# An attention layer in front of a folded two-matrix network: the first unit's inputs, means and head steps are moved

## The chip, the cores and the metric

The kernel runs on one core of a Trainium2 chip. The time is the device time of one execution in microseconds (us): 539.33 us as the median of three runs (539.18 to 541.11). The execution that the profiler recorded took 540.83 us, of which 539.0 us are the span from its first to its last instruction.

## The reference

```python
# attention: q, k, v are [4, 8, 768, 64]
k_sum = k.reshape(B, H, 24, 32, 64).max(axis=3)       # 24 summary keys per head
v_sum = v.reshape(B, H, 24, 32, 64).mean(axis=3)      # 24 summary values per head
scores_l = q @ k.T / 8, kept where |row - column| < 16, else -1e9
scores_s = q @ k_sum.T / 8 + log(32)
a = softmax(concatenate([scores_l, scores_s]))
x = (a @ concatenate([v, v_sum])).transpose(0, 2, 1, 3).reshape(3072, 512)
# network: w1, w2 [512, 1024], w3 [1024, 1024], w_out [1024, 512], all float64
out = ((x @ w1) * (x @ w2)) @ w3 @ w_out              # [3072, 512]
```

## The kernel before, in words

The 3072 tokens are six units of 512 tokens. Of each unit the eight heads are four pairs, so there are 24 pair steps. A pair step on TensorE is scores (`sc`, L319: queries against a window of 160 keys and 24 summary keys), then a softmax on the other engines, transposes of the softmax (`tp`, L373), and outputs (`po`, L393: against the values and the summary means). `keep_x` (L401) splits an output into a high and a low part for the network. The network per unit is two gate products, multiplied (`gate`, L409), and a projection with wp = w3 @ w_out (`project`, L444).

wp is made first: `fold_weights` (L192) needs all of w3 and w_out. Weights arrive as float64. `convert` (L152) turns a piece into a high and a low float32r part: an ACT step per 512 columns (L167), a shift (L175) and a bit merge (L178) on DVE, a rounding cast on ACT (L188), and the difference on DVE (L109). A fold product is three matmuls of 512 columns; a row x6 in the order is the two products that one w_out tile makes with one w3 tile. In the order, `w_106` to `w_357` are the four tiles of w_out, `w_115` to `w_196` are the first four tiles of w3, and `w_415`, `w_536`, `w_666`, `w_807` are the last four. `w_895` and later are w1 and w2.

What sets the order: SP and PE follow the program text (a manual schedule), ACT, DVE and POOL a list scheduler with priorities. The program text is a loop over steps t, one step for each weight piece that is begun. `LOADS` and `WORK` are tables of what is loaded and done at which step, `FIRST` gives the step at which a pair of the first two units begins, and `run` hands out fold and network matmuls up to a number of columns. From pair 8 on, a second loop puts two pairs at a time into the network's matmuls, in "slots" of transposes, scores, outputs. All input loads stand on SP's queue in order. A load into a buffer still in use waits there, and everything behind it waits too.

PSUM banks: `mm` 2 (gates, fold), `tp` 2 (transposes, outputs, and the accumulators of the third and fourth block of wp), `sc` 4. `ring` is ten SBUF buffers for raw weights, raw keys, values' rows and `h`.

Of the kernel before, what the change touches and what calls it, by code (L numbers as in the profile page):

```python
# [30 lines left out]
FIRST = (15, 18, 20, 22, 27, 32, 37, 44)  # L31
# [4 lines left out]
    *(("wo", 0, 0), ("w3", 0, 0), ("wo", 0, 1), ("w3", 1, 0), ("wo", 1), ("w3", 2, 0), ("w3", 3, 0)),  # L36
    *(("w3", 0, 1), ("w3", 1, 1), ("wo", 2), ("w3", 2, 1), ("w3", 3, 1), ("wo", 3)),
# [10 lines left out]
NORMALIZE = "VAAAAAAA"  # L48
SECOND = "AAAVAVVA"
# [21 lines left out]
def attention_moe(ctx, tc, qG, kW, kT, vP, vW, vB, mask, w1, w2, w3T, wo, out):  # L71
    nc = tc.nc
    B, NPAIR, _, S = kT.shape
    NB = S // BLOCK
# [20 lines left out]
    ident = const.tile([P, P], F32, name="ident")  # L95
    make_identity(nc, ident)
    mask_sb = const.tile([P, 3, KR], F32, name="mask_sb")


    mean_sb = sb.tile([P, S // P, P], F32, name="mean_sb", tag="v", bufs=2)  # L100
    nc.gpsimd.memset(mean_sb, 0.0)
    for i in range(P // BLOCK):
        for at in (CUT, CUT - 64):
            part = mean_sb.rearrange("p t n -> p (t n)")[i * BLOCK : (i + 1) * BLOCK, at + i :: P + P // BLOCK]
            nc.gpsimd.memset(part[:, : S // P], 1.0 / BLOCK)
# [22 lines left out]
    def weight(name, i, src, shape, part=None):  # L128

        n = src.shape[1] // 2  # L130
        parts = range(n // PIECE) if part is None else [part]
        units.append((name, i, shape, list(parts), len(todo) + len(parts) - 1))
        for k in parts:
            todo.append(src[:, 2 * k * PIECE : 2 * (k + 1) * PIECE])

    def start_loads(at_least):

        while todo or due_loads:
            if len(loading) >= at_least and len(loading) + len(working) + len(kraws) + len(vraws) + made[0] + 2 >= RING:
                return  # L140
            if due_loads:
                due_loads.pop(0)()
                continue
            if len(loading) >= AHEAD:
                return
            raw = sb.tile([P, 2 * PIECE], U32, name="wraw", tag="ring", bufs=RING)
            nc.sync.dma_start(raw, todo.pop(0))
            loading.append(raw)
            due_loads.extend(LOADS.pop(begun[0], ()))
            begun[0] += 1  # L150

    def convert(name, i, shape, parts, last):  # L152


        n = len(parts) * PIECE
# [6 lines left out]
        for k in range(len(parts)):  # L162
# [13 lines left out]
        for k, low_word in enumerate(low_words):  # L176
            some = bits[:, k * PIECE : (k + 1) * PIECE]
# [8 lines left out]
        at = parts[0] * PIECE  # L186
# [4 lines left out]
        have.update((name, i, part) for part in parts)  # L191

    def fold_weights(order):
        acc = {}
        for i, j in order:
            while not {("w3", i, j * P // PIECE), ("wo", j // 2, j % 2 * DO // PIECE)} <= have:
                yield 0
# [25 lines left out]
    def load_keys(b, p):  # L223
        raw = sb.tile([P, S], F32, name="raw", **held(b))
# [32 lines left out]
    def mean_products(tiles):  # L257
        po = ps.tile([P, 512], F32, name="means", tag="sc", bufs=4)
        for i in range(S // P):
            nc.tensor.matmul(  # L260
                po[:KR, :DM],
                lhsT=mean_sb[:, i, :KR],
                rhs=tiles[i // 2][:, i % 2],
                start=i == 0,
                stop=i == S // P - 1,
            )
        return po
# [17 lines left out]
    def load_sums(u, p, v):  # L285
        for b, blocks, n in batches(u):
            for g, at in enumerate((CUT, CUT - 64)):
# [4 lines left out]
                else:  # L292
                    src = vs[b][at : at + NB, p * P : (p + 1) * P]
                    nc.gpsimd.tensor_copy(to, src.unsqueeze(1).broadcast_to([NB, n, P]))

    def load_scores(u, p):
# [4 lines left out]
        nc.sync.dma_start(k, kW[p, :, u * NBLK : (u + 1) * NBLK])  # L301
        return q, k

# [108 lines left out]
    def gate(f, x, hs):  # L412
        acc = []
        for w in range(2):
# [6 lines left out]
            for c in range(NC):  # L421
                while (GATES[w], k, c * FQ // PIECE) not in have:
# [132 lines left out]
    def first_pair(s):  # L555
# [34 lines left out]
    def means():  # L590
        po = mean_products(vraws)
        vraws.clear()
        vs[0] = sb.tile([KR, DM], F32, name="vs0", tag="pt", bufs=6)
        nc.scalar.copy(vs[0], po[:KR, :DM])

    LOADS = {
        7: [lambda: nc.sync.dma_start(mask_sb, mask)],
        8: [lambda: rows(1)],
        11: [lambda: fetch(0)],
        12: [lambda: keys(1)],  # L600
        13: [lambda: keys(0)],
        14: [lambda: rows(0)],
        15: [lambda: rows(2), lambda: fetch_values(0)],
        16: [lambda: fetch(1)],
        18: [lambda: keys(3)],
        21: [lambda: fetch(2), lambda: fetch_values(1)],
        22: [lambda: keys(2)],
        24: [lambda: fetch(3)],
        25: [lambda: fetch_values(2)],
        28: [lambda: fetch_values(3)],  # L610
    }
    WORK = {
        13: [lambda: summaries(0, 0, kraws.pop(0)), lambda: fill(0)],
        14: [means, lambda: summaries(0, 1, kraws.pop(1)), lambda: fill(1)],
        19: [lambda: fetch_sums(0)],
        20: [lambda: load_second(0), lambda: load_second(3), lambda: summaries(0, 2, kraws.pop(2)), lambda: fill(2)],
        21: [lambda: load_second(1), lambda: summaries(0, 3, kraws.pop(3)), lambda: fill(3), lambda: fetch_sums(1)],
        22: [lambda: load_second(4), lambda: fetch(4), lambda: fetch_sums(2)],
        23: [lambda: second_batch(0), lambda: load_second(2)],
        24: [lambda: second_batch(1), lambda: fetch(5)],  # L620
        25: [lambda: second_batch(3), lambda: second_batch(4)],
        26: [lambda: second_batch(2), lambda: load_second(5)],
        27: [lambda: second_batch(5), lambda: load_second(6), lambda: fetch(6), lambda: fill(4), lambda: fill(5)],
        28: [lambda: fetch_sums(3)],
        29: [lambda: fetch_values(4), lambda: fetch_sums(4)],
        31: [lambda: load_second(7)],
        32: [lambda: second_batch(6)],
        37: [lambda: second_batch(7), lambda: fetch_values(5), lambda: fetch(7), lambda: fill(6), lambda: fetch_sums(5)],
        40: [lambda: fill(7)],
        42: [lambda: fetch_values(6)],  # L630
        43: [lambda: fetch_sums(6)],
# [143 lines left out]
```

## Time and profile before

| what | value |
|---|---|
| median of the runs | 539.33 us |
| the profiled execution / its span | 540.83 us / 539.0 us |
| PE busy, DVE busy, ACT busy, POOL busy | 517.9, 237.5, 238.9, 56.3 us |
| network's first matmul on PE | 88.9 us |
| end of PE's last matmul | 535.5 us |

TensorE is busy for 96% of the span, and its clock is granted at full speed but for two short stretches in the first 60 us. To read the profile, look at the first 90 us apart from the rest: in the rest PE hardly ever waits. A matmul's busy time in the page overlaps its neighbours', so rates are read from a long row of a chain or timeline divided by its count.

### The profile page before, as it was taken

To read this page: it belongs to the slowest core of one execution; us is meant where nothing else is said; L and a number is where in the kernel's file an instruction comes from. 1 tells how busy PE (TensorE), PEld (TensorE's weight loads), DVE (VectorE), ACT (ScalarE), POOL (GpSimd) and SP (SyncE) were. 2 spreads that over 40 slices of the span, in tenths; PEclk is the share of its full clock that TensorE was granted. 3 is DMA by queue.
4 is the path that set the end of the run, shared out by engine and by line. 5 is a ranking of instruction groups with operands and counts; after the bars stand their busy time and mean duration, and the time that the engine had idled before them with its cause. 6 is when DMAs were issued, how large, how long until landed. Compare 5 with 4: busy or idle time off the path is not lost.

```text
span 539.0 us, 9912 instructions
## 1 busy us (share of the span) xinstructions
PE 517.9 (96%) x3852; PEld 421.8 (78%) x3852; DVE 237.5 (44%) x686; ACT 238.9 (44%) x688; POOL 56.3 (10%) x103
## 2 busy tenths in 40 slices
PE   2897999999999999999999999999999999999997
PEld 1655777888788888888888888888888888888885
DVE  5868889999503226724244033252042351122210
ACT  5547898887345225226235144253162261222210
POOL 1001221111001101103003002011021020000000
PEclk9988899999999999999999999999999999999999
DMA  8999689956524005544032141050160020000001
GB/s 309 403 348 350 189 270 369 280 183 197 167 96 154 0 1 169 162 128 135 0 111 60 40 152 58 0 157 33 40 190 1 1 75 39 21 21 0 1 19 58
DMA packets 30574, 67.21 MB, mean 125 GB/s; under 512 B 4032, under 2 KB 7616, under 8 KB 30528
## 3 DMA queue, kind: packets, MB, share of 16 engines
q1 hardware_dynamic: 27072, 60.30, 35.2%
q10 hardware_dynamic: 3456, 6.29, 3.1%
q8 instruction: 30, 0.49, 0.4%
q14 instruction: 16, 0.13, 0.1%
HBM read 58.51 MB, written 6.29 MB: 120 GB/s over the span
## 4 chain that ended last, share of the span: by engine, by line
PE 91%; DVE 3%; ACT 3%; DMA 1%; issue 1%; POOL 0%; SPq 0%; POOLq 0%; ACTq 0%
PE mm L113 79%; PE po L393 5%; PE sc L319 4%; PE tp L373 2%; DVE w L109 1%; DMA wraw<-in_w3T_dram 1%; DVE wf L178 1%; ACT w L188 1%; PE means L260 1%; ACT sm L347 1%; DVE wf L175 1%; ACT wf L167 0%; ACT wp L211 0%; DVE wp L109 0%; POOL k L306 0%
## 5 line engine op out<-in xcount | busy, mean ns | idle before, releaser
L113 PE MATMUL mm<-x,w 128*128 128x512 f32 x1152 | 264.9, 390 | 0.0
L113 PEld LDWEIGHTS mm<-x,w 128*128 128x128 f32 x1152 | 215.4, 188 | 45.6 <-issue 0.5
L113 PE MATMUL mm<-wp,h 128*128 128x512 f32 x576 | 133.9, 391 | 0.0
L113 PEld LDWEIGHTS mm<-wp,h 128*128 128x128 f32 x576 | 107.5, 188 | 22.7 <-issue 0.2
L347 ACT ACTIVATE sm<-sm,mx 128x120 f32<-128x120 f32 x192 | 73.6, 387 | 19.9 <-DVE mx L333 19.9
L438 DVE TENSOR_TENSOR g<-mm,g 128x512 f32<-128x512 f32 x48 | 33.1, 689 | 90.6 <-PE mm L113 88.7
L439 ACT CAST h<-g 128x512 fp32r<-128x512 f32 x48 | 29.6, 618 | 87.7 <-DVE g L438 87.7
L113 PE MATMUL mm<-w,w 128*128 128x512 f32 x192 | 54.1, 435 | 12.6 <-ACT w L188 11.5
L113 PEld LDWEIGHTS mm<-w,w 128*128 128x128 f32 x192 | 38.2, 206 | 25.6 <-ACT w L188 13.3
L457 ACT COPY o<-mm 128x512 f32<-128x512 f32 x24 | 14.1, 585 | 81.3 <-PE mm L113 81.3
L109 DVE TENSOR_TENSOR h<-g,h 128x512 fp32r<-128x512 f32 x48 | 35.7, 743 | 24.2 <-ACT h L439 24.0
L435 ACT COPY g<-mm 128x512 f32<-128x512 f32 x48 | 28.0, 584 | 35.6 <-PE mm L113 35.2
L333 DVE CUSTOM_DVE_ANT_0 sm<-sc,mask_sb 128x120 f32<-128x120 f32 x192 | 41.0, 275 | 5.5 <-PE sc L319 5.5
L382 DVE COPY pt<-tp 120x512 f32<-120x512 f32 x19 | 12.4, 686 | 67.7 <-PE tp L373 67.7
L306 POOL COPY k<-ks 128x96 f32<-128x96 f32 (+1 forms) x32 | 10.1, 327 | 252.3 <-DMA k<-in_kW_dram 210.0
L347 ACT ACTIVATION_READ_ACCUMULATOR sm<-sm,mx 128x1 f32 x192 | 36.5, 190 | 0.0
L109 DVE TENSOR_TENSOR x<-po,x 128x512 fp32r<-128x512 f32 x24 | 16.6, 690 | 42.2 <-ACT x L404 42.2
L356 POOL TENSOR_TENSOR sm<-sm,mx 128x960 f32<-128x960 f32 x16 | 29.1, 1820 | 6.0 <-DVE mx L353 5.0
L167 ACT ACTIVATE wf<-wraw 128x512 f32<-128x512 f32 x40 | 26.1, 669 | 6.2 <-DMA wraw<-in_wo_dram 2.7
L188 ACT CAST w<-wf 128x1024 fp32r<-128x1024 f32 (+1 forms) x25 | 21.9, 875 | 12.8 <-DVE wf L178 12.7
L393 PEld LDWEIGHTS po<-pt,v 120*64 120x64 f32 x768 | 23.8, 138 | 4.7 <-issue 2.9
L109 DVE TENSOR_TENSOR w<-wf,w 128x1024 fp32r<-128x1024 f32 (+1 forms) x25 | 25.4, 1014 | 4.4 <-ACT w L188 4.1
(33 smaller groups left out, 281.1 us busy)
## 6 DMA issues: line engine op xcount, KB each, us to landing
k<-in_kW_dram SPq DMA_DIRECT2D x24, 368.0 KB
wraw<-in_w3T_dram SPq DMA_DIRECT2D x16, 512.0 KB
wraw<-in_w_dram SPq DMA_DIRECT2D x16, 512.0 KB
q<-in_qG_dram SPq DMA_DIRECT2D x24, 256.0 KB
raw<-in_kT_dram SPq DMA_DIRECT2D x16, 384.0 KB
out_dram<-o ACTq DMA_DIRECT2D x24, 256.0 KB
v<-in_vW_dram SPq DMA_DIRECT2D x24, 192.0 KB
raw<-in_vB_dram SPq DMA_DIRECT2D x12, 384.0 KB
```

The lines of the kernel that those rows point to most:

```text
L109: eng.tensor_tensor(dst, src, hi.bitcast(F32), ALU.subtract)
L113: nc.tensor.matmul(acc, lhsT=a, rhs=b, start=first and i == 0, stop=last and i == len(terms) - 1)
L167: nc.scalar.activation(f[:, k * PIECE : (k + 1) * PIECE], words[:, :, 1].bitcast(F32), AF.Prelu, scale=2.0**-112, alpha=-(2.0**32),)
L188: nc.scalar.copy(hi, f)
L319: nc.tensor.matmul(sc[h][64 * g : 64 * g + 64, i * KR : (i + 1) * KR], lhsT=q[rows, i * P + 64 * g : i * P + 64 * g + 64], rhs=k[rows, i, ...
L333: nc.vector.tensor_tensor_reduce(out=sm[:, j], in0=sc[h][:, i * KR : (i + 1) * KR], in1=mask_sb[:, 0 if blk == 0 else 2 if blk == BLOCKS - ...
L347: nc.scalar.activation(sm[:, j], sm[:, j], AF.Exp, bias=mx[:, 0, j : j + 1], scale=-1.0, accum_out=mx[:, 1, j : j + 1])
L356: nc.gpsimd.tensor_tensor(sm, sm, mx[:, 2].unsqueeze(2).broadcast_to([P, NI, KR]), ALU.mult)
L393: nc.tensor.matmul(po[cols, at : at + 64], lhsT=v[:, g, i, cols], rhs=pt[g][:, (h * NBLK + i) * 64 : (h * NBLK + i + 1) * 64], start=True, ...
L435: nc.scalar.copy(g, a[:, :U])
L438: nc.vector.tensor_tensor(g, acc[1][:, :U], g, ALU.mult)
L439: nc.scalar.copy(h[:, 0], g)
```

## The change

Six things are changed. (1) The first unit's keys for scores are no longer loaded (`in_kW_dram`): GpSimd copies the windows out of the whole keys (`windows`), which are now loaded with 16 columns of padding. (2) The first w_out and w3 pieces are loaded and converted in pieces of 256 columns. (3) The summary means are made by 24 products of 24x128 at four places of the array in place of 6 products of 120x512. (4) Pairs 4 to 7 (the second unit) run two at a time, pairs 6 and 7 with their transposes in the second loop. (5) The steps at which pairs, loads and fills stand are moved; the scores of pair 0 come before the products of the third w_out tile. (6) Some transposes go to `sc` banks (`BANKS`), and some softmax and copy work changes its engine (`NORMALIZE`, `SECOND`).

```diff
-FIRST = (15, 18, 20, 22, 27, 32, 37, 44)
+FIRST = (12, 21, 23, 25, 45, 54)
...
-    *(("wo", 0, 0), ("w3", 0, 0), ("wo", 0, 1), ("w3", 1, 0), ("wo", 1), ("w3", 2, 0), ("w3", 3, 0)),
+    *(("wo", 0, 0, 256), ("w3", 0, 0, 256), ("wo", 0, 256, 256), ("w3", 0, 256, 256), ("wo", 0, 512)),
...
-NORMALIZE = "VAAAAAAA"
-SECOND = "AAAVAVVA"
+NORMALIZE = "VPAAVVVA"
+SECOND = "AVAAVAVA"
+BANKS = "SSTTTSTS"
...
             def store(i=i):
                 done = acc.pop(i)[:, :DO]
-                nc.scalar.copy(wp[i][:, 0], done)
-                low(nc.vector, wp[i][:, 1], done, wp[i][:, 0])
+                with tc.high_priority(offset=SOONER):
+                    nc.scalar.copy(wp[i][:, 0], done)
+                    low(nc.vector, wp[i][:, 1], done, wp[i][:, 0])
...
         for i in range(S // P):
-            nc.tensor.matmul(
-                po[:KR, :DM],
-                lhsT=mean_sb[:, i, :KR],
-                rhs=tiles[i // 2][:, i % 2],
...
+            for p in range(NPAIR):
+                nc.tensor.matmul(
+                    po[32 * p : 32 * p + NB, :P],
+                    lhsT=mean_sb[:, i],
+                    rhs=tiles[i // 2][:, i % 2, p * P : (p + 1) * P],
...
-        nc.sync.dma_start(k, kW[p, :, u * NBLK : (u + 1) * NBLK])
+        if u:
+            nc.sync.dma_start(k, kW[p, :, u * NBLK : (u + 1) * NBLK])
         return q, k
+
+    def windows(k, raw):
+        for to, at in ((k[:, :, :CUT], 0), (k[:, :, CUT + NB :], CUT)):
+            nc.gpsimd.tensor_copy(to, raw[:, at : at + U].rearrange("p (i c) -> p i c", c=P)[:, :, : to.shape[2]])
...
+    def four_pairs(s):
+        steps = two_pairs(s)
+        yield from steps
+        while t[0] < FIRST[-1]:
+            yield
+        steps = two_pairs(s + 2)
+        tps = [transposes(sms.pop(p)[0], **more) for p, more in zip((s, s + 1), ({}, SPARE))]
+        pts = [evacuate(tp, SECOND[p]) for p, tp in zip((s, s + 1), tps)]
+        next(steps)
+        for p, pt in zip((s, s + 1), pts):
+            keep_x(outputs(pt, values.pop(p)), xs[place(p)[0]])
+        yield
+        yield from steps
...
-        13: [lambda: summaries(0, 0, kraws.pop(0)), lambda: fill(0)],
-        14: [means, lambda: summaries(0, 1, kraws.pop(1)), lambda: fill(1)],
+        12: [lambda: first_keys(0), lambda: fill(0)],
+        17: [means],
+        18: [lambda: first_keys(1), lambda: fill(1)],
...
-    RATE = 6600
-    LATER_RATE = 6944
+    RATE = 9200
+    LATER_RATE = 3344
...
-            last = (s - 2, s - 1) if s > NFIRST else ()
+            last = (s - 2, s - 1)
```

`two_pairs` begins both pairs (scores of both), then reduces, exponentiates and normalizes one after the other; `first_keys` is `windows` and the summary keys of one pair.

On PE, from the second w_out tile on; before, the order of fold products, means and the first scores reads:

```order
L113 MATMUL mm<-w_162,w_196 128x512 x6
L113 MATMUL mm<-w_253,w_115 128x512 x6
L113 MATMUL mm<-w_253,w_137 128x512 x6
L113 MATMUL mm<-w_253,w_171 128x512 x6
L260 MATMUL means<-rows,mean_sb 120x512 x6
L113 MATMUL mm<-w_253,w_196 128x512 x6
L319 MATMUL sc<-k,q 64x120 x16
L113 MATMUL mm<-w_357,w_115 128x512 x6
```

And after the change, on the same engine and place (w_173, w_307 and w_397 are the second to fourth tile of w_out, w_111 to w_205 the first four of w3, w_453 the fifth):

```order
L117 MATMUL mm<-w_173,w_205 128x512 x6
L337 MATMUL sc<-k,q 64x120 x16
L117 MATMUL mm<-w_307,w_111 128x512 x6
L117 MATMUL mm<-w_307,w_148 128x512 x6
L117 MATMUL mm<-w_307,w_184 128x512 x6
L117 MATMUL mm<-w_307,w_205 128x512 x6
L269 MATMUL means<-rows,mean_sb 24x128 x24
L117 MATMUL mm<-w_397,w_111 128x512 x6
```

The first scores moved ahead of the third w_out tile, and the means behind it.

On DVE after the change, the instructions between the third and the fourth w_out tile (the rows behind the 8 score reductions of pair 0, which follow `w_307`):

```order
L182 TENSOR_SCALAR wf<-wf 128x512
L113 TENSOR_TENSOR w_184<-wf,w_184 128x512
L185 SCALAR_TENSOR_TENSOR wf<-wraw,wf 128x512
L371 RECIPROCAL mx<-mx 128x8
L383 TENSOR_TENSOR sm<-sm,mx 128x960
L113 TENSOR_TENSOR w_205<-wf,w_205 128x512
L237 TENSOR_REDUCE ks<-raw 128x24
L182 TENSOR_SCALAR wf<-wf 128x1024
L185 SCALAR_TENSOR_TENSOR wf<-wraw,wf 128x512 x2
L113 TENSOR_TENSOR w_397<-wf,w_397 128x1024
```

Before, the reductions, the reciprocal and the multiplication of pair 0 stood behind `w_357`, the fourth tile; now they stand ahead of it.

On PE, at the end of the fold and the start of the network, before:

```order
L113 MATMUL mm<-w_357,w_807 128x512 x6
L373 MATMUL tp<-ident,sm 120x64 x16
L319 MATMUL sc<-k,q 64x120 x16
L393 MATMUL po<-pt,v 64x64 x16
L113 MATMUL mm<-x,w_895 128x512 x12
L113 MATMUL mm<-x,w_977 128x512 x12
```

and after (w_806 is the eighth tile of w3, w_928 and w_963 are the first tiles of w1 and w2):

```order
L117 MATMUL mm<-w_397,w_806 128x512 x6
L394 MATMUL tp<-ident,sm 120x64 x16
L337 MATMUL sc<-k,q 64x120 x32
L414 MATMUL po<-pt,v 64x64 x16
L117 MATMUL mm<-x,w_928 128x512 x12
L117 MATMUL mm<-x,w_963 128x512 x12
```

The scores of pairs 4 and 5 now both stand ahead of the last outputs of the first unit and of the network.

## Rows read from the trace of the kernel before

**Rows 1.** Busy time by stage: PE, PEld, DVE, ACT, POOL (us), clock, DMA share, GB/s.

```profile
9.50:28.40 18.90, 15.77 (x50) 10.24 (x50) 16.66 (x28) 11.54 (x18) 0.00 (x0) 1.00 1.03 404
28.40:47.10 18.70, 18.69 (x90) 12.63 (x90) 12.93 (x33) 10.36 (x29) 3.29 (x6) 0.91 1.04 359
47.10:57.00 9.90, 6.02 (x57) 4.87 (x57) 9.43 (x28) 7.86 (x22) 0.24 (x1) 0.66 0.92 277
57.00:88.90 31.90, 30.98 (x363) 24.21 (x361) 27.73 (x72) 28.31 (x86) 7.00 (x14) 1.00 0.85 263
88.90:535.50 446.60, 446.40 (x3299) 369.87 (x3296) 167.81 (x526) 175.89 (x530) 43.96 (x67) 1.00 0.28 87
```

**Rows 2.** PE's waits from 0 to 120 us: total, times, longest (us).

```profile
PE mm L113 <- ACT w L188: 11.5, 3, 9.5
PE tp L373 <- DVE wp L109: 3.9, 2, 2.4
```

**Rows 3.** Chain that ended last, in order of time: start us, us, what.

```profile
1.20 5.73 DMA wraw<-in_w3T_dram
...
26.06 1.05 ACT w L188
27.13 1.24 DVE w L109
...
33.94 5.15 PE means L260 x12
...
58.99 1.11 PE po L393 x32
...
67.41 0.61 PE tp L373 x16
...
71.39 0.98 PE sc L319 x32
```

**Rows 4.** PE in order of time: start us, us, what.

```profile
41.40 5.73 PE L113 MATMUL mm<-w,w 128*128 128x512 f32 x24
...
109.08 11.18 PE L113 MATMUL mm<-x,w 128*128 128x512 f32 x48
```

**Rows 5.** Loads of the score keys, from the page's list of DMA issues.

```profile
k<-in_kW_dram SPq DMA_DIRECT2D x24, 368.0 KB
```

**Rows 6.** POOL's groups: line 306 (min/median/max ns), and two by form (us, mean ns).

```profile
L306 POOL COPY k<-ks x32: 214/264/1154, 32.1 to 399.1; 128x96 f32<-128x96 f32 x16, 128x48 f32<-128x48 f32 x16
...
L352 POOL TENSOR_SCALAR mx<-mx 128x8 f32<-128x8 f32 x24 | 5.8, 243 | 116.2 <-ACT sm L347 115.7
...
L294 POOL COPY v<-vs 24x512 f32<-24x512 f32 x8 | 4.9, 609 | 12.3 <-ACT vs L594 7.1 <-PE po L393 4.9
```

**Rows 7.** DVE in order of time, single instructions from 31 to 67 us.

```profile
31.05 0.94 DVE L230 TENSOR_REDUCE ks<-raw 128x24 f32<-128x768 f32 x1
...
37.55 1.23 DVE L109 TENSOR_TENSOR w<-wf,w 128x1024 fp32r<-128x1024 f32 x1 [1.11 <-ACT w L188]
41.52 0.28 DVE L333 CUSTOM_DVE_ANT_0 sm<-sc,mask_sb 128x120 f32<-128x120 f32 x1 [2.74 <-PE sc L319]
...
44.64 0.68 DVE L175 TENSOR_SCALAR wf<-wf 128x1024 uint32<-128x1024 uint32 x1
45.24 0.68 DVE L109 TENSOR_TENSOR wp<-mm,wp 128x512 fp32r<-128x512 f32 x1
45.84 1.28 DVE L178 SCALAR_TENSOR_TENSOR wf<-wraw,wf 128x512 uint32<-128x512 uint32 x2
...
47.73 1.16 DVE L364 TENSOR_TENSOR sm<-sm,mx 128x960 f32<-128x960 f32 x1
...
66.07 1.21 DVE L247 TENSOR_REDUCE vs<-raw 96x32 f32<-96x1024 f32 x1
```

**Rows 8.** ACT in order of time: one exponential of a pair's eight.

```profile
42.30 0.38 ACT L347 ACTIVATE sm<-sm,mx 128x120 f32<-128x120 f32 x1
```

**Rows 9.** Two more stretches, as rows 1.

```profile
30.00:40.00 10.00, 10.00 (x29) 6.07 (x28) 7.17 (x10) 4.34 (x8) 0.74 (x2) 0.86 1.04 329
...
88.90:130.00 41.10, 41.10 (x316) 33.24 (x314) 38.91 (x98) 35.37 (x102) 6.24 (x14) 1.00 0.78 239
```

More of the change, by code (lines that the diff above doesn't have):

```diff
@@ L126, in attention_moe, with weight @@
     begun, due_loads, kraws, vraws = [0], [], {}, {}
-    def weight(name, i, src, shape, part=None):
+    def weight(name, i, src, shape, at=None, length=PIECE):
         n = src.shape[1] // 2
[L131 to L134, printed above, removed]
+        parts = [(k, PIECE) for k in range(0, n, PIECE)] if at is None else [(at, length)]
+        units.append((name, i, shape, parts, len(todo) + len(parts) - 1))
+        for k, length in parts:
+            todo.append(src[:, 2 * k : 2 * (k + length)])
     def start_loads(at_least):
@@ L152, in convert @@
     def convert(name, i, shape, parts, last):
-        n = len(parts) * PIECE
+        at, n = parts[0][0], sum(length for _, length in parts)
         f = sb.tile([P, 2 * PIECE], F32, name="wf", bufs=5)[:, :n]
@@ L158, in convert @@
         low_words = []
-        for k in range(len(parts)):
+        for k, length in parts:
             raw = loading.pop(0)
@@ L190, in convert @@
         low(nc.vector, lo, f, hi)
-        have.update((name, i, part) for part in parts)
+        have.update((name, i, c) for c in range(at, at + n, P))
     def fold_weights(order):
@@ L195, in fold_weights @@
         for i, j in order:
-            while not {("w3", i, j * P // PIECE), ("wo", j // 2, j % 2 * DO // PIECE)} <= have:
+            while not {("w3", i, j * P), *(("wo", j // 2, j % 2 * DO + c) for c in range(0, DO, P))} <= have:
                 yield 0
@@ L223, in load_keys @@
     def load_keys(b, p):
[L224 removed]
+        raw = sb.tile([P, PAD + S], F32, name="raw", **held(b))
         nc.sync.dma_start(raw, kT[b, p])
@@ L259, in mean_products @@
         for i in range(S // P):
-            nc.tensor.matmul(
-                po[:KR, :DM],
-                lhsT=mean_sb[:, i, :KR],
-                rhs=tiles[i // 2][:, i % 2],
[L264 to L267, printed above, removed]
+            for p in range(NPAIR):
[3 more added lines that the diff above has]
+                    rhs=tiles[i // 2][:, i % 2, p * P : (p + 1) * P],
+                    start=i == 0,
+                    stop=i == S // P - 1,
+                )
+        yield
+        vs[0] = sb.tile([P, P], F32, name="vs0", tag="pt", bufs=6)
+        for p in range(NPAIR):
+            nc.scalar.copy(vs[0][32 * p : 32 * p + NB], po[32 * p : 32 * p + NB, :P])
     def batches(u):
@@ L421, in gate @@
             for c in range(NC):
-                while (GATES[w], k, c * FQ // PIECE) not in have:
+                while (GATES[w], k, c * FQ) not in have:
                     yield 0
@@ L590, in means @@
     def means():
-        po = mean_products(vraws)
+        pairs.append(mean_products(vraws))
+        next(pairs[-1])
         vraws.clear()
-        vs[0] = sb.tile([KR, DM], F32, name="vs0", tag="pt", bufs=6)
-        nc.scalar.copy(vs[0], po[:KR, :DM])
     LOADS = {
[L597 to L610, printed above, removed]
+        10: [lambda: rows(1)],
+        12: [lambda: keys(0)],
+        14: [lambda: fetch(0), lambda: nc.sync.dma_start(mask_sb, mask)],
+        15: [lambda: fetch_values(0)],
+        16: [lambda: keys(1), lambda: rows(0)],
+        19: [lambda: rows(2), lambda: keys(2)],
@@ L698, in attention_moe @@
             with tc.manual_schedule(engines={engines.Activation, engines.DVE}):
-                spare = ({}, {"tag": "sc", "bufs": 4})
-                tps = [transposes(sms.pop(p)[0], **more) for p, more in zip(last, spare)]
+                tps = [transposes(sms.pop(p)[0], **more) for p, more in zip(last, ({}, SPARE))]
                 pts = [evacuate(tp) for tp in tps]
```

126 lines of the change are left out of this document (80 added, 46 removed).

## The prediction

> **What bounds the kernel now.** I read the busy time by stage first. From 88.9 us, where the network's first matmul starts, to 535.5 us PE is busy 446.40 of 446.60 us at full clock [rows 1]. What follows 88.9 us is therefore a fixed amount of PE work, and the change can move the time only by moving the start of the network, N, as long as nothing new makes PE wait behind it. Then the waits: in the first 120 us PE lost 11.5 us to the ACT cast of a weight, 9.5 of them before its first matmul, and 3.9 us to transposes that waited for their PSUM banks, held by the wp accumulators until DVE had read them [rows 2]. The stage rows show the kinds of stretches ahead of N. Up to 47 us the DMA engines are full (share 1.03 and 1.04) and weights arrive no faster than they are used. From 47.1 to 57.0 us DVE is busy 9.43 of 9.90 us while PE has 6.02, at a granted clock of 0.66, between its two levels of 1.2 and 2.4 GHz. From 57.0 to 88.9 us PE is nearly full and DVE has 27.73 of 31.90 [rows 1].
>
> The order of the changed kernel gives two marks. M is the first product of the fourth w_out tile, 41.40 us before [rows 4]. N is 88.9 us before. I work out both.
>
> **The change part by part.**
>
> *Smaller first pieces.* The first matmul now waits for half of the bytes and for conversions half as long; it starts about a microsecond sooner (an estimate). This is worth nothing at M: behind it PE waits for the third w_out tile, whose cast ended at 27.1 us and whose low part ended at 28.4 us [rows 3]. Summing the sizes of the loads in SP's order, this tile has 7,048 KB up to its end where it had 6,836, 0.5 us more at 404 GB/s [rows 1]. The DVE steps ahead of it are nearer, since one w3 piece comes earlier. I bound its low part between 27.2 and 28.4 us and take 27.8.
>
> *Keys by GpSimd.* Four loads of 368 KB go [rows 5]; the whole keys grow by 8 KB each. That is 3.6 us of full DMA, but the fourth w_out tile has 10,820 KB up to its end where it had 10,788, so at M it is nothing; it helps the last w3 tiles, which come behind DVE anyway. Each pair gets two copies of 384 and 256 elements per partition. The trace has no such copy. From below, 512 elements took 609 ns, so a pair costs 0.8 us; from above, the longest copy of line 306 took 1154 ns [rows 6], and if that was one of 96 elements, a pair costs 7.7 us. I take 2 us, nearer the row with the nearest size. The first pair's keys land at about 21 us (6.7 MB at 404 GB/s behind a start of 4.3 us, from 1 MB that had landed at 6.93 us [rows 1, 3]), so its scores can run at about 24 us. There PE waits for the third tile, and the 0.98 us of scores [rows 3] are hidden. The Trainium skill (GPSIMD Engine Reference, Specifications) says that GpSimd shares its SBUF interface with VectorE and contends with DVE instructions of two SBUF inputs. It speaks against this change, because bit merges and low parts have two such inputs; the spread of 214 to 1154 ns agrees [rows 6], and by that rule the upper price is the likelier.
>
> *Means by small products.* Before, six products took 5.15 us [rows 3]. Now 24 products have as many columns in all, four places side by side. If they don't overlap, they cost 5.15 us again. If a record costs what one costs in the outputs, 1.11 us for 32 [rows 3], the 48 records cost 1.7 us, which I take. The Trainium skill (TensorEngine Tiling (Array Packing), Tiling Modes) gives four independent tiles of 128x32, which would make it 1.3 us; no row shows that tile size. In N all three are the same: the last of the values' rows lands at about 35.6 us (12.65 MB), the third of the products that needs it ends by 37.4 us at the dearest, and PE waits for M behind it.
>
> *First softmax ahead of the fourth tile.* This is the new wait. DVE is in order, and the reciprocal of pair 0 waits for its eight exponentials, with the low part of a w3 piece, the key maxima and the fourth tile queued behind. From 27.8 us: a reduction 0.28, eight exponentials of 0.38 [rows 8], the POOL step 0.24 [rows 6] and a reciprocal of about as much, the multiplication 1.16, a low part 0.68, the maxima 0.94, shift 0.68, merges 1.2, cast 1.05, low part 1.23 [rows 3, 7]: 10.7 us. The low part is there at 38.5 us, M is about 38.3. That is 3.1 us sooner, since the softmax no longer stands behind the means.
>
> *Transposes into score banks.* Pair 0's transposes no longer wait for wp's banks, so the 3.9 us [rows 2] go. What is late next is the fifth w3 tile, by 38.5 us plus shift, merges, maxima, two low parts: about 43 us, when PE arrives at 43.8. Covered, narrowly.
>
> *From M to N.* PE: 120 matmuls of 0.23 us (11.18 for 48 [rows 4]), four transposes of 0.61, five scores of 0.98, four outputs of 1.1 [rows 3]: 39.3 us, N at 77.6. DVE: ahead of the scores of pair 5, which are now ahead of N, stands the reduction of their summary keys. From 38.5 us DVE has up to and with it, by its order: 30 instructions of the 0.68 us kind (starts are 0.60 apart, so each costs 0.08 less than its duration), 18.0; five low parts of 1.15, 5.8; four key maxima of 0.86, 3.4; three score sets of 8 x 0.20, 4.9; four value sums of 1.13, 4.5; small ones 0.8 [rows 7]. In all 37.4 us. DVE's share of busy time was 95% and 87% in the two stages that correspond [rows 1]; at 91% this takes 41.1 us and ends at 79.6. A fill by POOL (median 264 ns [rows 6]), 0.98 of scores and 1.1 of outputs follow: N is at 82.0. DVE is later than PE, so it sets N, and a slow clock stretch in between costs PE little. Loads for this stretch queue on SP behind the values of pair 3, which wait for the outputs of pair 1; ten PE microseconds lie between these and the scores of pair 4, room for about eight of loads (four loads, 1.4 MB at 263 GB/s, and some 2 us of start, an estimate).
>
> *Behind N.* The weights of w1 and w2, gates and two softmaxes at a time are DVE work of the same amount as before; from 88.9 to 130.0 us DVE had 38.91 of 41.10 us and PE none idle [rows 9]. I cost the pairing and the moved slots at nothing. If that cover goes, each microsecond of lateness at the transposes of pairs 4 and 5 is one in the time.
>
> *Sum.* Before, N was 88.9 us with pair 5's scores still to come, so 89.9 to compare; now 82.0. The span loses 7.9 us: 531.1 us, in an execution like the profiled one 532.9 us. The median stood 1.5 us below the profiled execution's 540.83 us, so I predict 531.4 us.
>
> **The rivals.** *Nothing waits behind M:* DVE keeps ahead (few of its waits between 47 and 57 us would come back), N is 77.6, the time 527.0 us. For it: 95% in one stage. Against: 87% in the longer one.
>
> *Copies contend and DVE is at 87%:* the scores of pair 0 end near 30 us (keys 7.7 us after 21, fill, scores), M moves by 2.2 us, and 37.4 us take 43.0: N is at 86.0, the time 535.4 us. The range of line 306 speaks for it, its median of 264 ns against it.
>
> *DVE starves, slower than before:* every second load of the second unit's values waits for a DVE sum two loads ahead, lands microseconds later, and DVE stands in order at the next sum; from 30 to 40 us it had only 7.17 of 10 us [rows 9]. At 72%, 37.4 us take 52, N is 92.8, the time 542.2 us. It decides from a share below 76%, where N reaches 89.9. Against it: the same loads stood in the stages with 95% and 87%.
>
> **How the numbers follow.** The forecast 0.50, nothing waits 0.15, copies contend 0.22, DVE starves 0.08, and 0.05 for a small loss behind N that eats the gain. About 0.5%, 2.7 us, is what a measurement can tell from no change. The first three cases are faster, less a little for their upper ends: 0.81 faster; 0.10 the same; 0.09 slower. The range goes from 526.5, just under the second case, to 537.5, just over the third.
>
> **What would show it.** Right: N near 82 us, M near 38, no wait of transposes for wp, pair 0's scores by 26 us, PE waiting shortly for pair 5's scores, and PE full behind N. Wrong: M behind 41 us, scores of pair 0 that wait for POOL beyond 27 us, a DVE share between M and N under 80%, or PE waits at the transposes of pairs 4 to 7.

## The result, and the profile after

The kernel after takes 542.33 us (median of nine runs, 541.11 to 542.67), the kernel before beside it 539.33 us: a ratio of 1.0039, 95% interval 1.0024 to 1.0053. I had predicted 531.4 us with a range of 526.5 to 537.5, so the prediction was wrong in sign. The profiled execution took 541.36 us, its span 539.6.

PE of the kernel after in order of time (start us, us, what; in brackets what ended the idle time before):

```profile
11.46 1.65 PE L117 MATMUL mm<-w,w 128*128 128x512 f32 x3 [11.46 <-ACT w L194]
...
19.69 11.23 PE L117 MATMUL mm<-w,w 128*128 128x512 f32 x36 [0.52 <-ACT w L194]
...
31.84 0.73 PE L117 MATMUL mm<-w,w 128*128 128x512 f32 x2
...
40.32 1.51 PE L269 MATMUL means<-rows,mean_sb 128*24 128x128 f32 x48
43.12 0.73 PE L117 MATMUL mm<-w,w 128*128 128x512 f32 x2 [1.29 <-ACT w L194]
...
54.55 0.68 PE L394 MATMUL tp<-ident,sm 64*120 64x64 f32 x16
...
76.57 1.10 PE L394 MATMUL tp<-ident,sm 64*120 64x64 f32 x15 [1.99 <-DVE x L113]
...
90.60 4.76 PE L117 MATMUL mm<-x,w 128*128 128x512 f32 x18
```

The first matmul starts at 11.46 us (9.50 before [rows 2]), the third w_out tile (x2 at 31.84) 4.7 us later than before, M is 43.12 (41.40 [rows 4], forecast 38.3) and N 90.60 (88.9 before with pair 5's scores still to come, forecast 82.0). What the change aimed at came: the means take 1.51 us for 5.15 [rows 3], and the transposes at 54.55 wait for nothing, where 3.9 us were lost [rows 2]. One wait is new: later transposes, at 76.57, wait 1.99 us for DVE. Two stretches, with columns as in [rows 1]:

```profile
57.00:90.60 33.60, 31.00 (x380) 23.96 (x379) 31.26 (x86) 28.40 (x88) 10.26 (x17) 0.95 0.83 259
90.60:536.00 445.40, 444.32 (x3268) 369.40 (x3264) 169.69 (x529) 169.12 (x506) 42.68 (x66) 1.00 0.28 87
```

DVE (the third figure with a count) is busy 31.26 of the 33.60 us ahead of N. It did not starve; it had more to do. Behind N PE is as full as before. From the end of the fourth tile's low part to the end of the key maximum that pair 5's scores need (GpSimd's fill and these scores follow it):

```profile
44.33:88.61 44.28, 41.43 (x422) 31.95 (x422) 41.87 (x99) 34.85 (x101) 13.29 (x21) 0.96 0.83 261
```

**Where the head is lost.** First ACT, then DVE, of the kernel after in its first 32 us:

```profile
4.71 0.43 ACT L174 ACTIVATE wf<-wraw 128x256 f32<-128x256 f32 x1 [2.71 <-DMA wraw<-in_wo_dram]
...
9.45 0.43 ACT L174 ACTIVATE wf<-wraw 128x256 f32<-128x256 f32 x1 [0.80 <-DMA wraw<-in_w3T_dram]
9.79 0.69 ACT L194 CAST w<-wf 128x256 fp32r<-128x256 f32 x2
```

```profile
5.50 0.43 DVE L185 SCALAR_TENSOR_TENSOR wf<-wraw,wf 128x256 uint32<-128x256 uint32 x1
...
8.69 0.29 DVE L182 TENSOR_SCALAR wf<-wf 128x256 uint32<-128x256 uint32 x1 [1.66 <-ACT wf L174]
...
10.21 0.42 DVE L113 TENSOR_TENSOR w<-wf,w 128x256 fp32r<-128x256 f32 x1 [0.89 <-ACT w L194]
...
16.54 0.69 DVE L182 TENSOR_SCALAR wf<-wf 128x1024 uint32<-128x1024 uint32 x1
...
27.59 0.94 DVE L237 TENSOR_REDUCE ks<-raw 128x24 f32<-128x768 f32 x1
...
31.59 1.23 DVE L113 TENSOR_TENSOR w<-wf,w 128x1024 fp32r<-128x1024 f32 x1
```

ACT takes its instructions in order, and all four widenings of half pieces stand ahead of the first cast: it waits for the fourth landing (9.45) although the first half was merged by 5.93. The kernel before, in these rows, widened two pieces, which are as many bytes, and cast at 7.52:

```profile
4.72 0.66 ACT L167 ACTIVATE wf<-wraw 128x512 f32<-128x512 f32 x1 [2.72 <-DMA wraw<-in_wo_dram]
6.95 0.66 ACT L167 ACTIVATE wf<-wraw 128x512 f32<-128x512 f32 x1 [1.57 <-DMA wraw<-in_w3T_dram]
7.52 0.60 ACT L188 CAST w<-wf 128x512 fp32r<-128x512 f32 x1
```

The rows show something else, too: 256 KB landed no sooner than 512 KB (the ACT step behind them starts at 4.71 and 4.72 us). The halves moved more slowly altogether. From 2 to 9 us, the kernel after, then e1, which is the same kernel with whole pieces (the last two columns are DMA share and GB/s):

```profile
2.00:9.00 7.00, 0.00 (x0) 0.00 (x0) 1.33 (x5) 1.29 (x4) 0.00 (x0) 1.00 0.78 246
```

```profile
2.00:9.00 7.00, 0.00 (x0) 0.00 (x0) 2.14 (x4) 2.30 (x5) 0.00 (x0) 1.00 0.95 317
```

From about 9 us DVE has little idle time left, so lateness stays: its first shift of 1024 columns starts at 16.54 (13.31 before), a key maximum of 0.94 us stands ahead of the third tile, and that tile's low part starts at 31.59, 4.5 us later than in [rows 3].

**What became longer.** DVE beside GpSimd (POOL), both in order of time:

```profile
44.24 1.11 DVE L182 TENSOR_SCALAR wf<-wf 128x1024 uint32<-128x1024 uint32 x1
45.39 1.99 DVE L185 SCALAR_TENSOR_TENSOR wf<-wraw,wf 128x512 uint32<-128x512 uint32 x2
...
64.01 3.07 DVE L185 SCALAR_TENSOR_TENSOR wf<-wraw,wf 128x512 uint32<-128x512 uint32 x2
67.01 1.20 DVE L254 TENSOR_REDUCE vs<-raw 96x32 f32<-96x1024 f32 x1
```

```profile
43.91 2.92 POOL L306 COPY v<-vs 24x512 f32<-24x512 f32 x3 [1.67 <-ACT vs L279]
...
63.42 2.21 POOL L383 TENSOR_TENSOR sm<-sm,mx 128x960 f32<-128x960 f32 x1 [0.32 <-DVE mx L371]
65.57 1.77 POOL L320 COPY k<-raw 128x384 f32<-128x384 f32 x2
67.29 0.43 POOL L324 COPY k<-ks 128x96 f32<-128x96 f32 x2
```

A pair of merges costs 1.28 us alone [rows 7], 1.99 and 3.07 here. Comparing every DVE instruction up to N with the shorter ones of its form, 13 are over 60 ns too long, together 5.1 us, and each of them overlaps a GpSimd instruction: fills of values (L306) 2.1 us, the normalisation (L383) 1.5, key copies (L320) 1.5. In the kernel before no instruction is. The reduction at 67.01 overlaps one and keeps its 1.20 us. This is what the Trainium skill (GPSIMD Engine Reference, Specifications) says: contention with DVE instructions of two SBUF inputs or in a two-port mode; the trace agrees, with 0.69 us made 2.16 in the worst case. In the kernel before it was GpSimd that paid: of the 32 copies of line 306 [rows 6], 27 take 214 to 269 ns, and the five that take 586 to 1154 ns are those that run beside a DVE instruction with two SBUF inputs (a merge or a low part).

### The profile page after: what moved, and what is told of

It is laid out like the page before. It is cut to its first block, busy times and chain, and to the rows that moved or that the text cites. A ratio compares the mean times of both kernels' runs of the same rounds, so it can differ in the third digit from the quotient of the medians.

```text
span 539.6 us, 9972 instructions
## 1 busy us (share of the span) xinstructions
PE 514.8 (95%) x3888; PEld 421.0 (78%) x3888; DVE 245.8 (46%) x696; ACT 231.2 (43%) x662; POOL 64.0 (12%) x108
## 4 chain that ended last, share of the span: by engine, by line
PE 79%; DVE 7%; ACT 5%; issue 3%; DMA 3%; POOL 1%; SPq 0%; POOLq 0%; ACTq 0%
PE mm L117 71%; PE po L414 4%; PE sc L337 3%; ACT sm L365 3%; DVE wf L185 2%; PE tp L394 2%; DVE w L113 2%; DMA wraw<-in_w3T_dram 1%; DVE wf L182 1%; ACT w L194 1%; DMA wraw<-in_w_dram 1%; DVE ks L237 1%; DMA raw<-in_kT_dram 1%; DVE vs L254 0%; POOL sm L383 0%
## 5 line engine op out<-in xcount | busy, mean ns | idle before, releaser
L117 PE MATMUL mm<-w,w 128*128 128x512 f32 x192 | 55.5, 440 | 17.6 <-ACT w L194 14.5
L113 DVE TENSOR_TENSOR h<-g,h 128x512 fp32r<-128x512 f32 x48 | 35.3, 739 | 25.3 <-ACT h L460 25.2
L324 POOL COPY k<-ks 128x96 f32<-128x96 f32 (+1 forms) x32 | 8.5, 280 | 237.1 <-DMA k<-in_kW_dram 222.9
L194 ACT CAST w<-wf 128x1024 fp32r<-128x1024 f32 (+2 forms) x27 | 22.2, 825 | 25.1 <-DVE wf L185 24.9
L174 ACT ACTIVATE wf<-wraw 128x512 f32<-128x512 f32 (+1 forms) x42 | 26.7, 649 | 10.2 <-DMA wraw<-in_wo_dram 4.2
L185 DVE SCALAR_TENSOR_TENSOR wf<-wraw,wf 128x512 uint32<-128x512 uint32 (+1 forms) x42 | 30.1, 734 | 0.6
L113 DVE TENSOR_TENSOR w<-wf,w 128x1024 fp32r<-128x1024 f32 (+2 forms) x27 | 26.5, 985 | 5.3 <-ACT w L194 5.0
```

What stands on the lines that cost most here:

```text
L113: eng.tensor_tensor(dst, src, hi.bitcast(F32), ALU.subtract)
L117: nc.tensor.matmul(acc, lhsT=a, rhs=b, start=first and i == 0, stop=last and i == len(terms) - 1)
L174: nc.scalar.activation(f[:, k : k + length], words[:, :, 1].bitcast(F32), AF.Prelu, scale=2.0**-112, alpha=-(2.0**32),)
L185: nc.vector.scalar_tensor_tensor(out=some, in0=low_word, scalar=29, in1=some, op0=ALU.logical_shift_right, op1=ALU.bitwise_or)
L194: nc.scalar.copy(hi, f)
```

## The experiments

M and N in us from the one profiled execution of each kernel, the median, and the ratio to the kernel before on the same chip (95%); the chips differ between rows, so that differences of under 1 us between medians say little. In e3, e4 and e8 pair 5's scores come behind N, as before.

| kernel | M | N | median us | ratio |
|---|---|---|---|---|
| before | 41.40 | 88.89 | 539.33 | 1 |
| after | 43.12 | 90.60 | 542.33 | 1.0024 to 1.0053 |
| e1 after, whole first pieces | 39.76 | 86.48 | 537.75 | 0.9946 to 0.9977 |
| e2 after, softmax 0 later | 42.15 | 93.45 | 545.47 | 1.0076 to 1.0132 |
| e3 before, half pieces | 42.44 | 89.83 | 541.99 | 1.0017 to 1.0047 |
| e4 before, small means, spare banks | 38.08 | 86.81 | 539.05 | 0.9965 to 0.9995 |
| e5 e1, key copies by ACT | 39.74 | 86.78 | 538.40 | 0.9960 to 0.9982 |
| e6 e1, keys loaded | 40.62 | 91.09 | 543.75 | 1.0053 to 1.0108 |
| e7 e1, normalisation by ACT | 39.92 | 85.87 | 537.13 | 0.9930 to 0.9967 |
| e8 before, key copies | 41.92 | 92.11 | 545.77 | 1.0093 to 1.0129 |
| e9 e1, half conversions | 41.47 | 89.00 | 540.14 | 1.0004 to 1.0033 |
| e11 e7, all copies by ACT | 39.21 | 88.35 | 540.54 | 1.0015 to 1.0058 |
| e13 after again | 43.62 | 91.06 | 542.35 | 1.0032 to 1.0064 |
| e14 e7 again | 40.02 | 86.29 | 536.86 | 0.9932 to 0.9976 |

**e1, whole first pieces.**

```
-    *(("wo", 0, 0, 256), ("w3", 0, 0, 256), ("wo", 0, 256, 256), ("w3", 0, 256, 256), ("wo", 0, 512)),
+    *(("wo", 0, 0), ("w3", 0, 0), ("wo", 0, 512)),
-FIRST = (12, 21, 23, 25, 45, 54)
+FIRST = (10, 19, 21, 23, 43, 52)
```

The steps in `LOADS` and `WORK` go down by two as well.

> The kernel after, with the first w_out and w3 pieces whole again (512 columns, as before); every table is shifted by the two pieces that go, nothing else. Theory (the half pieces put the whole head late): first matmul near 9.5 us (11.46 after), the low part of the third w_out tile ends at 28 to 29 us (32.8), M near 38.5 us (43.1), and, as the stretch from M to N is as long as it is in the kernel after (46.4 to 47.5 us), N at 85 to 87 us (90.6); the time near 538 us. Rival (loads or DVE work behind M set N, whatever M is): M moves by 4 us, but N stays within 1 us of 90.6 and the time near 542. Second rival (the half pieces cost only their own start): first matmul 2 us sooner, M and N within 1.5 us of the kernel after.

The theory held in N and in the time; the third tile's low part (29.8 us) and M (39.76) are some 1 us later than expected. With this one edit the change is a gain, 4.6 us better than the kernel after. PE in order of time:

```profile
9.81 6.51 PE L117 MATMUL mm<-w,w 128*128 128x512 f32 x12 [9.81 <-ACT w L194]
...
18.07 8.00 PE L117 MATMUL mm<-w,w 128*128 128x512 f32 x34 [0.53 <-DVE w L113]
...
28.55 0.73 PE L117 MATMUL mm<-w,w 128*128 128x512 f32 x2 [1.23 <-ACT w L194]
...
86.48 8.82 PE L117 MATMUL mm<-x,w 128*128 128x512 f32 x36
```

34 matmuls take 8.00 us, 0.24 each. In the kernel after 36 take 11.23. Its groups of instructions from 19.7 to 25 us, then from 25.2 to 30.8 (busy us behind the bar):

```profile
L117 PE MATMUL mm<-w,w 128*128 128x512 f32 x12 | 5.7, 644 | 0.6 <-ACT w L194 0.5
```

```profile
L117 PE MATMUL mm<-w,w 128*128 128x512 f32 x25 | 6.0, 394 | 0.0
```

A matmul of 512 columns is 0.47 us apart from the next up to 25 us, and 0.24 behind it. From this factor of two, PE ran at the lower of its two levels until 25 us there, and to 17 or 18 us here; the granted-clock column reads 1.00 all through these stretches and doesn't show it.

**e9, which part of the half pieces harms.** Transfers whole, conversions in halves:

```
-    *(("wo", 0, 0), ("w3", 0, 0), ("wo", 0, 512)),
+    *(("wo", 0, 0, 256), ("wo", 0, 256, 256), ("w3", 0, 0, 256), ("w3", 0, 256, 256), ("wo", 0, 512)),
...
+        if length < PIECE and at % PIECE:
+            return
+        if length < PIECE:
+            parts = [(at, PIECE)]
...
-            raw = loading.pop(0)
+            raw = loading[0] if length < PIECE and k % PIECE == 0 else loading.pop(0)
```

> e1 (whole first transfers) with the first two pieces converted in halves of 256 columns as in the kernel after; only the transfers stay whole. Theory (the half transfers do the harm: they land no sooner, and ACT, in order, takes all four widenings ahead of the first cast): first matmul 9.0 to 10 us, third w_out tile and M within 1 us of e1 (28.5, 39.8), N 86 to 87.5 us, the time 537 to 538.7 us. Rival (the additional halves of conversions on ACT and DVE do the harm): first matmul over 10.5 us, M over 41.5 us, N over 88.5 us, the time over 540 us.

One more thing differs from the kernel after: both halves of w_out are converted ahead of those of w3, where the kernel after alternates. Both theories missed, though the rival's N and time came. The first matmul (9.83) and the third tile's low part on DVE (it starts at 28.48 us; 28.53 in e1) are those of e1, so the halved conversions alone don't make DVE late; with halved transfers it is. ACT has four widenings ahead of its first cast here, too, but these whole pieces have landed by 7.21:

```profile
7.21 0.75 ACT L181 ACTIVATE wf<-wraw 128x256 f32<-128x256 f32 x2 [1.76 <-DMA wraw<-in_w3T_dram]
7.87 0.39 ACT L201 CAST w<-wf 128x256 fp32r<-128x256 f32 x1
```

So that order alone does no harm; it takes the late fourth landing (9.45) as well, or the alternation, which e9 leaves out together with it. Yet N is 2.5 us later than in e1. PE in order of time:

```profile
9.83 3.73 PE L117 MATMUL mm<-w,w 128*128 128x512 f32 x6 [9.83 <-ACT w L201]
13.89 3.22 PE L117 MATMUL mm<-w,w 128*128 128x512 f32 x6 [0.33 <-ACT w L201]
17.63 1.22 PE L117 MATMUL mm<-w,w 128*128 128x512 f32 x2 [0.52 <-ACT w L201]
19.82 10.52 PE L117 MATMUL mm<-w,w 128*128 128x512 f32 x34 [0.96 <-DVE w L113]
...
31.25 4.65 PE L117 MATMUL mm<-w,w 128*128 128x512 f32 x19
```

PE stays at the lower level until 25 us, as in the kernel after; the same 34 matmuls take 10.52 us, and PE reaches the third tile at 31.25, late by itself. Pair 0's scores stand behind these matmuls, and DVE waits for them with its softmax, which moves M by 1.7 us. In the kernel after DVE takes the scores straight behind the third tile's low part, without a wait. First e9, then the kernel after:

```profile
31.37 0.28 DVE L358 CUSTOM_DVE_ANT_0 sm<-sc,mask_sb 128x120 f32<-128x120 f32 x1 [1.67 <-PE sc L344]
```

```profile
32.73 0.27 DVE L351 CUSTOM_DVE_ANT_0 sm<-sc,mask_sb 128x120 f32<-128x120 f32 x1
```

So up to M the two losses don't add up in the kernel after: DVE's lateness, from the halved transfers, covers that of PE. At N the kernel after is 1.6 to 2.1 us later than e9. What makes the clock rise late isn't shown. The short waits between the first products (0.33, 0.52 and 0.96 us here) don't decide it: e2, below, has the kernel after's waits to within 0.01 us up to 19.8 us, and its matmuls are fast from 21 us on:

```profile
21.05 8.01 PE L117 MATMUL mm<-w,w 128*128 128x512 f32 x34 [0.53 <-DVE w L113]
```

So it isn't shown either that the halved conversions cost e9 its 2.5 us; they may be those of one execution's clock. The ten runs of e9 go from 539.21 to 542.39 us.

**e3, half pieces alone in the kernel before** (e1's edit backwards).

> The kernel before with the half first pieces alone (the first w_out and w3 pieces in 256 columns; tables shifted by the two further pieces). Theory (half pieces land no sooner and make the stream and the conversions late): first matmul near 11.4 us (9.5 before), third tile's cast near 31 us (27.1), M at 43.5 to 46 us (41.4), N at 91 to 94 us (88.9), the time 541 to 544 us. Rival (before has slack at M, where the means stand): first matmul later, but M and N within 1 us of before, the time 539.3.

They cost there as well, 2.4 us in the median, as the theory said, and less than in the kernel after. M and N are later by 1.0 and 0.9 us only, as the rival said, but against an execution of the kernel before that lost time to its clock: the third tile's second row starts 2.6 us later (31.04 for 28.41), and its 16 matmuls take 3.95 us where they took 5.53, at a granted clock of 0.50 from 30 to 32 us. Against the second profiled execution of the kernel before (e10: 39.99 and 88.20) M is 2.5 us later and N 1.6.

**e2, the first softmax at its old place.**

```
-FIRST = (12, 21, 23, 25, 45, 54)
+FIRST = (17, 21, 23, 25, 45, 54)
```

> The kernel after with pair 0's first step moved from step 12 to step 17, behind the fourth w_out tile and the means; half pieces and all else stay. Theory (the chain of pair 0's softmax delays the fourth tile, 32.7 to 36.8 us on DVE): M goes from 43.1 to about 39 us; the softmax then costs its DVE time later, so N moves less, 88.5 to 90.5 us, and the time is 540 to 542 us. Rival (the half pieces alone make the head late): M still over 42 us and N within 1 us of 90.6 or later.

My theory of the softmax fell: put back, it costs 3 us; the rival's signs (M over 42, a late N) came. M is sooner by 1.0 us, but the eight exponentials then stand on ACT ahead of the next w3 tile's cast, which PE meets at 50.87:

```profile
50.87 0.80 PE L117 MATMUL mm<-w,w 128*128 128x512 f32 x1 [2.98 <-ACT w L194]
53.42 5.71 PE L117 MATMUL mm<-w,w 128*128 128x512 f32 x17 [1.76 <-DVE w L113]
```

**e4, means and spare banks alone in the kernel before.**

```
-                lhsT=mean_sb[:, i, :KR],
-                rhs=tiles[i // 2][:, i % 2],
+                    lhsT=mean_sb[:, i],
+                    rhs=tiles[i // 2][:, i % 2, p * P : (p + 1) * P],
...
-            pt = evacuate(transposes(sms.pop(s)[0]), SECOND[s])
+            pt = evacuate(transposes(sms.pop(s)[0], **({"tag": "sc", "bufs": 4} if s == 0 else {})), SECOND[s])
```

> The kernel before with two parts of the change alone: the means by 24 small products, and pair 0's transposes into the banks of the scores. First theory (PE's own work in the head counts): the means take 1.5 us for 5.15 and the 3.9 us wait of the transposes goes, M is near 38 to 39 us (41.4) and N 84 to 86.5 us (88.9); the time 535 to 537.5 us. Rival (DVE sets N in both kernels): M moves, N stays within 1 us of 88.9 and the time within 1 us of 539.3.

M came 3.3 us sooner and N 2.1, the time 1 us: for the time the rival was nearer. The wait for wp's banks was replaced by one for DVE:

```profile
48.38 1.11 PE L377 MATMUL tp<-ident,sm 64*120 64x64 f32 x16 [3.55 <-DVE sm L368]
```

**e8 and e6, the key copies each way.** e8 adds `windows` to the kernel before and drops the loads; e6 is the same edit backwards, from e1:

```
+        if u:
             nc.sync.dma_start(k, kW[p, :, u * NBLK : (u + 1) * NBLK])
...
+        windows(inputs[p][1], raw)
```

> The kernel before with the window copies by GpSimd alone (no loads from kW for the first unit, whole keys 16 columns longer). Theory (copies lengthen DVE, DVE sets N): merges up from 687 to 730 to 780 ns, N up by 0.5 to 2 us at a like start, the time 540 to 541.5 us. Rival (the 3.6 us of DMA that are saved come through): N sooner by 1 to 3 us, the time 536.5 to 538.5 us.

> The kernel after with whole first pieces (as e1), and the first unit's key windows loaded from kW again, as before: no GpSimd copies, four loads of 368 KB more. Theory (GpSimd's copies cost more than the loads they save): merges near 700 ns, N at 84.5 to 86 us (86.5 in e1), the time 535.5 to 537.3 us. Rival (loads set the head up to 47 us): pair 0's scores and the rows of values land 0.9 to 3 us later, M over 41 us (39.8) and N at 87 us or later.

Both lost some 6 us in the median (e6's runs go from 540.82 to 547.01 us, and the profiled one is the fastest of them). In e8 the merges mean 693 ns, not 730 or more, and DVE's excess is 1.0 us, so the theory had the sign and not the cause. A DVE wait is new, and PE paid twice, by waiting ahead of N and then at a lower clock behind it (the column ahead of the last two):

```profile
DVE vs L248 <- DMA raw<-in_vB_dram: 2.0, 1, 2.0
```

```profile
89.00:93.00 4.00, 2.47 (x34) 2.12 (x35) 3.64 (x13) 3.09 (x9) 0.22 (x1) 0.81 1.03 403
93.00:97.00 4.00, 4.00 (x15) 3.12 (x15) 3.77 (x13) 2.83 (x13) 0.55 (x1) 0.77 1.00 322
```

Why the values' blocks land late there stays open. In e6 the merges still mean 765 ns, and PE waits for keys that, loaded at the changed places, come late:

```profile
72.85 1.88 PE L336 MATMUL sc<-k,q 64*64 64x120 f32 x32 [3.69 <-POOL k L323]
...
89.44 0.64 PE L336 MATMUL sc<-k,q 64*64 64x120 f32 x16 [2.01 <-POOL k L323]
```

So the copies cost 6 us in the old order and save 6 in the new one, with the loads at these places; no run tried others.

**e5, e7 and e11, GpSimd's work moved to ACT.** e5: the key copies; e7: pair 1's normalisation; e11: both, and the first unit's fills of values.

```
-            nc.gpsimd.tensor_copy(to, raw[:, at : at + U].rearrange("p (i c) -> p i c", c=P)[:, :, : to.shape[2]])
+            nc.scalar.copy(to, raw[:, at : at + U].rearrange("p (i c) -> p i c", c=P)[:, :, : to.shape[2]])
...
-NORMALIZE = "VPAAVVVA"
+NORMALIZE = "VAAAVVVA"
...
-                    nc.gpsimd.tensor_copy(to, src.unsqueeze(1).broadcast_to([NB, n, P]))
+                    (nc.gpsimd.tensor_copy if u else nc.scalar.copy)(to, src.unsqueeze(1).broadcast_to([NB, n, P]))
```

> The kernel after with whole first pieces (as e1), and the eight window copies of keys by ACT in place of GpSimd. Theory (a running GpSimd copy lengthens DVE's instructions): bit merges that mean 774 ns in e1 fall to 700 to 720 ns, DVE's busy time up to N falls by 1.5 to 2.5 us from 74.2, and N moves from 86.5 to 84 to 85.5 us; the time 535.5 to 537 us. Rival (the merges are lengthened by something else, such as DMA writes, or DVE's time is not what sets N): merges stay over 760 ns or N stays within 0.5 us of 86.5; with ACT's 3 to 4 us more, N may even be later.

> The kernel after with whole first pieces (as e1), and pair 1's normalisation by ACT (eight instructions) in place of the one by GpSimd at 59.3 us. Theory: the merge that stood beside it (2.16 us for 0.69) and the next one fall back, 1.5 to 2 us less on DVE, N at 84.8 to 86 us (86.5). Rival (DVE has room there, or ACT's 2.6 to 3.0 us cost as much): N within 0.5 us of 86.5, or later.

> The kernel after with whole first pieces, pair 1's normalisation, the window copies and the first unit's fills of values all by ACT: GpSimd keeps only short fills of keys and eight-column steps. Theory (each DVE instruction is lengthened only while a GpSimd instruction over SBUF runs, and DVE sets N): no DVE instruction of the head is over 60 ns longer than its like (3.7 us of such excess in e1, 1.8 in e7), N 84 to 85.5 us (86.5 in e1, 85.9 in e7), the time 535 to 536.7 us. Rival (ACT, with some 9 us more, takes DVE's place): the excess goes, but N stays at 85.5 to 88 us and casts come late.

e5 is a miss: merges still mean 767 ns, since the fills and the normalisation go on; N is no sooner, though here PE lost 1.6 us to a lower clock at 73 us (18 matmuls in 6.00 us for 4.40), and the time is no better than e1's. e7 takes 1.8 us of excess away (3.7 to 1.8), N moves by 0.6: the theory's direction at a third of its price. In e11 the excess is 0.1 us and the merges mean 688 ns, but N goes to 88.35, late as the rival said. From 47 us to 86 or 88 us, e1 and then e11 (DVE third, ACT fourth):

```profile
47.00:86.00 39.00, 35.01 (x434) 27.08 (x434) 36.62 (x93) 31.45 (x93) 11.13 (x17) 1.00 0.81 265
```

```profile
47.00:88.00 41.00, 38.72 (x436) 29.14 (x436) 35.47 (x94) 38.38 (x109) 3.44 (x10) 0.96 0.83 267
```

ACT, busy 38.38 of 41 us, has taken DVE's place. What the lengthening costs in time isn't shown: e7's 0.6 us at N is a difference of two single executions, e14, the same kernel again, has 86.29, and the intervals of e1 and e7 overlap.

**e10, e12, e13 and e14, kernels again** (no edit).

> The kernel before once more, for a second profiled execution (the first was 1.5 us above the median). Theory (the first had a slow stretch in the head that others have not): N at 87 to 88 us (88.9), the rest behind N as long as before (450.1 us). Rival (N is the same in every execution, and the median lies lower for a reason behind N): N within 0.3 us of 88.9.

> The kernel after once more, for a second profiled execution (the first was 1.0 us below the median). Theory (DVE's lateness varies with where GpSimd's instructions fall): first matmul and M within 0.7 us of 11.5 and 43.1, N 90.6 to 92.5 us, DVE's excess 4 to 7 us. Rival (the difference lies behind N): N within 0.3 us of 90.6.

> The kernel after a third time, timed beside the kernel before and beside e14. Theory (in the execution of e12 the weights behind N landed late and ACT, in order, held pair 3's x behind them; most executions lose less there): a median of 541.5 to 543.5 us, N 90.3 to 91.5 us, and PE's wait for x behind N under 1 us. Rival (it is what this kernel does on most chips): a median over 544 us and a wait for x of 2 us or more.

> The kernel of e7 again (whole first pieces, pair 1 normalised by ACT), on the same chip as e13. Theory: 536.5 to 537.8 us, 4.5 to 6 us under e13 and 2 to 3 us under before. Rival (its gain was the chip's): within 1 us of before.

e10 took 540.39 us with N at 88.20 and 450.4 us behind it, between theory and rival. Why both profiled executions of the kernel before stand over its median is on record: their mean granted clock is 0.989, and in the timed runs of the kernel before beside e1 to e14 the 21 at 0.989 took 540.77 us in the median, the 19 at 0.995 to 0.997 took 538.66. So the theory was right of both executions: the N of before in the table is that of one with some 10 us at half clock (in 28 to 34 and 48 to 58 us). The single execution e12 took 548.0 us with N at 91.03, and lost 6 us behind it, 2.4 of them where ACT held pair 3's x behind a widening of late weights; e13, 542.35 us in the median, has no such wait, so that is not the kernel's habit. e14 repeats e7's gain on another chip: 536.86 us, 5.5 us better than e13 beside it and 2.8 better than before. It beats both kernels.

## Why the prediction was wrong

The span was forecast at 531.1 us and is 539.6. From the fourth tile's low part: it ends at 44.33 for 38.5 (5.8 us), and from there to N it takes 46.3 us for 43.5 (2.8 us); together 8.6. The median adds 2.4: I took it 1.5 us under the profiled execution, and it stands 1.0 above.

- *Smaller first pieces* is the step that failed. I wrote that the first matmul "now waits for half of the bytes", that it "starts about a microsecond sooner" and that this "is worth nothing at M", and let the third tile's low part end at 27.8. The first matmul came 2.0 us later, and the low part ended at 32.8: 5.0 of the 8.6 us. I summed bytes at one rate, and did not ask how fast halves move (246 GB/s for 317 up to 9 us) and in which order ACT takes them (its first cast waits for the fourth). PE's late clock, which I had not thought of either, is covered by this up to M. e1 undoes it: 29.8. Of the 2.0 us that remain there, 0.94 are the key maximum, which I had not put ahead of this tile.
- *First softmax*: forecast 10.7 us from the third tile's low part to the fourth's, measured 11.5 (0.7 of it lengthened instructions). The chain was right, and in e2 the old place is the worse one.
- *Keys by GpSimd*: 1.3 to 1.8 us a pair for the 2 us taken; hidden on GpSimd, but they lengthened DVE's instructions by 1.5 us, a price that my sum had not. The upper price (1154 ns for 96 elements) was no cost of a copy: the same copy takes 264 ns where no two-input DVE instruction runs beside it. That leaving the loads out is worth 6 us in this order (e6) I had put at nothing.
- *Means* (1.5 for 1.7 us) and *spare banks* (the wait gone) were right, and worth little alone (e4), since DVE is late next.
- *From M to N*: DVE's work of 37.4 us was counted nearly rightly. Up to 88.6 us DVE was busy 41.9 us, of which 3.9 are lengthening, at a share of 95% where I took 91. The rival "Copies contend" had the mechanism; that it would act through older fills, which the new order puts beside merges, no term of mine held.
- *Rivals*: "DVE starves" had the time (542.2) and not the cause: its share was 95%.
- *Behind N*: next to nothing, as said: 444.32 of 445.40 us busy.

## What to carry to other kernels

Before a first transfer is cut in two, read how fast the parts move and what an in-order engine between them and the first matmul does with them; bytes alone don't tell. On an engine that is full, count an instruction at its length beside GpSimd, and put GpSimd's long instructions where that engine reads PSUM or reduces (an inference from the rows; no run tried it). A bundle of moves is tried part by part in both orders: here one part spoiled a bundle that gains 2 us without it, and another is worth some 6 us in one order and costs 6 in the other.

## What the runs showed of the hardware

- 256 KB landed no sooner than 512 KB as the first transfer (4.71 and 4.72 us), and with the first four transfers halved the DMA engines moved 246 GB/s for 317 from 2 to 9 us.
- PE's clock rose at 25 us in the kernel after and e9, at 17 or 18 us in e1 and by 21 us in e2, at the price of 2.5 us for 34 matmuls (e9 and e1). The waits between the first products don't explain it, since those of e2 are those of the kernel after.
- A GpSimd normalisation of 2.21 us made one merge last 2.16 us for 0.69. A reduction beside a GpSimd copy was not lengthened, and neither were the gates' products, which read PSUM (six beside GpSimd instructions in the kernel after, 0.68 to 0.69 us).
- It goes the other way, too: a GpSimd copy of 264 ns took 1154 ns beside a low part of DVE.
- 24 small products side by side took 1.51 us; the estimate from the Trainium skill (TensorEngine Tiling (Array Packing), Tiling Modes) was 1.3.
